# Second MoE product with w_out stationary, 144 tokens moving, and results turned by VectorE

## The chip, the cores and the metric

The kernel runs on one core of one Trainium2 chip. The metric is device microseconds (us) of one execution, and lower is better. A kernel is executed several times, always beside the kernel before on the same chip, and medians with their ranges are given. One execution of each kernel is profiled. Everything is fp32.

## The reference

Attention over pooled keys and values feeds a two-layer product, which the program calls `moe` (hence the title). Cut to what matters:

```python
# q, k, v: 8 batches x 8 heads x 576 x 64; k and v are averaged over 8 rows
attn = softmax(q @ k_p.T / 8);  x = (attn @ v_p) as (4608 tokens, 512)
h = x @ w_in                       # 512 x 2048: the first product
s = sin(alpha * h)
g = h + s * s / (alpha + 1e-9)
out = g @ w_out                    # 2048 x 512: the second product
```

The change concerns the last line, and how `g` and `w_out` are laid out for it.

## The kernel before

Both products use a two-level scheme of seven products in place of eight: a block product is split into 7 outer products of sums of blocks, each of these into 7 inner ones. Words used below:

- A **unit** is the piece of tokens that the second product finishes before it starts the next: 512 tokens, so 9 units.
- A **step** is one outer product: 7 inner products with four fp32 matmuls each. The profile shows two TensorE instructions per matmul, so a step has 56 and a unit 392.
- **Outer sums** are additions over whole 128x2048 blocks of `g`, four per unit. **Inner sums** are additions over quarters of such a block, four per step. VectorE makes both.
- The **bridge** is the buffer in HBM through which `g` goes from the first product to the second.

The data are stationary (first operand of `matmul`), 128 columns of weights move, and the outputs have tokens on partitions:

```python
def outer(u, n):                       # u: unit, n: step in it
    ...
    if n == 1: x[5] = new(5); tt(flat(x[5]), flat(r["r21"]), flat(x[4]), OP.add)
    if n == 2:
        x[6] = new(6); tt(flat(x[6]), flat(x[5]), flat(x[1]), OP.subtract)
        x[7] = r["r21"]; tt(flat(x[7]), flat(x[1]), flat(x[7]), OP.subtract)
    if n == 3: x[3] = new(3); tt(flat(x[3]), flat(x[2]), flat(x[6]), OP.subtract)

def inner(u, p):                       # the four inner sums of a step, made one step ahead
    ...
    tt(s1, a(2, 1), a(2, 2), OP.add)
    tt(s2, s1, a(1, 1), OP.subtract)   # product 6 of the step reads s2
    tt(s4, a(1, 2), s2, OP.subtract)
    tt(s3, a(1, 1), a(2, 1), OP.subtract)

def product(st, q, out, start):
    A, W = st["A"][q], self.W[st["p"]][q]
    for J in range(self.NJ):
        nc.tensor.matmul(out, A[:, J, :], W[:, J // 2, J % 2, :], ...)
...
for k in range(len(seq) + 1):          # one step; the order in which TensorE meets its products
    ...
    product(st, 1, yz[:, 0, :], True)
    ...                                # products 5 and 4 of the step before
    product(st, 6, x[:, 1, :], False)
    ...                                # products 2 and 3 of the step before, then its combination
    product(st, 7, x[:, 2, :], False)
...
self.load_g(0, ("r21",))
with tc.manual_schedule(engines={nc.tensor.engine}):   # only TensorE keeps the written order;
    for _ in o:                                        # a scheduler orders the other engines
        pass
```

A finished output block of 256 tokens x 256 columns goes to HBM in one store with rows of 1 KB.

Of the kernel before, what the change touches and what calls it, by code (L numbers as in the profile page):

```python
# [40 lines left out]
class Kernel:  # L41
    def __init__(self, tc, q, k, v, w_in, w_out, alpha, out):
        self.tc, self.nc = tc, tc.nc
        self.q, self.k, self.v = q, k, v
        self.w_in, self.w_out, self.alpha, self.out = w_in, w_out, alpha, out
        self.B, self.H, self.S, self.D = q.shape
        self.Sp = self.S // POOL
        self.DM = self.H * self.D
        self.FF = w_in.shape[1]
        self.K1 = self.DM // P  # L50
        self.K2 = self.FF // P
        self.NP = self.H // 2
        self.NU = self.B * self.S // (2 * TH)
        self.NJ = self.K2 // 2 // JW
        self.xT = {}
        self.gd = self.nc.dram_tensor("g_bridge", (self.NU, self.NJ, P, 4 * JW * TH), F32, kind="Internal").ap()

    def home(self, i, shape):

        return self.xp.tile(shape, F32, name=f"home{i}")  # L60
# [319 lines left out]
    def load_w_out(self, wp):  # L380


        nc, h, kk = self.nc, self.DM // 2, self.K2 // 2
        src = self.w_out.rearrange("(k p) n -> p k n", p=P)
        self.wb = {p: wp.tile([P, self.NJ, 2, 2, P], F32, name=f"wb{p}") for p in range(1, 8)}
        flat = lambda t: t[:].rearrange("p a b c d -> p (a b) (c d)")
        b11, b21, b22, t4, t1, t2, b12 = (flat(self.wb[p]) for p in range(1, 8))
        for t, i, j in ((b11, 0, 0), (b12, 0, 1), (b22, 1, 1), (b21, 1, 0)):
            nc.sync.dma_start(out=t, in_=src[:, i * kk:(i + 1) * kk, j * h:(j + 1) * h])
        for c in range(0, kk, 2):  # L390
            yield
# [7 lines left out]
        self.W = {}  # L399
# [5 lines left out]
    def inner_w(self, p, wp):  # L405
# [11 lines left out]
        tt(t1, b(1, 2), b(1, 1))  # L417
        tt(t2, b(2, 2), t1)
        tt(b(1, 2), b(2, 2), b(1, 2))
        tt(t4, b(2, 1), t2)  # L420
        self.W[p] = {1: b(1, 1), 2: b(2, 1), 3: b(2, 2), 4: t4, 5: t1, 6: t2, 7: b(1, 2)}

# [24 lines left out]
    def hidden(self, u, extra):  # L447
# [5 lines left out]
        for slot in range(7 * self.NJ):  # L453
# [5 lines left out]
            if k == 0:  # L459
                before = self.group  # L460
                G = self.group = SimpleNamespace(
                    u=u, J=J, b1=bank(), g=self.hp.tile([P, 2, 2, JW, TH], F32, name="h"),
                    s=self.hp.tile([P, 2, 2, JW, TH], F32, name="s", bufs=1))
# [11 lines left out]
            def sin(G, i, j, src):  # L475
                for jj in range(JW):
                    f = i * self.K2 // 2 + G.J * JW + jj
                    nc.scalar.activation(out=G.s[:, i, j, jj, :], in_=src[:, jj, :], func=AF.Sin, scale=self.al[:, f:f + 1])  # L478

            def square(G, i, js):  # L480

                for jj in range(JW):
                    f = i * self.K2 // 2 + G.J * JW + jj
                    x = G.s[:, i, js, jj, :]
# [33 lines left out]
            def left4(G=G):  # L518
                add(G.g[:, 1, 1], G.b7[:], G.p5[:])

            def left5(G=G):
                add(G.g[:, 0, 1], G.b6[:], G.p5[:])
                sin(G, 1, 1, G.g[:, 1, 1])
                add(G.g[:, 0, 0], G.b1[:], G.s[:, 0, 0])

            def left6(G=G):
                sin(G, 0, 1, G.g[:, 0, 1])
# [10 lines left out]
    def finish(self, Q):  # L538
        add = lambda o, x, y: self.nc.vector.tensor_tensor(out=o, in0=x, in1=y, op=OP.add)  # L539
        add(Q.g[:, 1, 0], Q.b7[:], Q.s[:, 1, 0])  # L540
        add(Q.g[:, :, 1], Q.g[:, :, 1], Q.s[:, :, 1])

    def store_g(self, Q):
        self.nc.sync.dma_start(out=self.gd[Q.u, Q.J], in_=Q.g[:].rearrange("p a b c d -> p (a b c d)"))
# [142 lines left out]

    def load_g(self, u, names):
        for n in names:
            i, j = divmod(("r11", "r12", "r21", "r22").index(n), 2)  # L690
            shape = [P, self.NJ, JW, 2, P]
            t = self.home(0 if n == "r22" else 2, shape) if n in ("r22", "r21") else self.gp.tile(shape, F32, name=n)
            self.nc.sync.dma_start(out=t[:].rearrange("p J a b c -> p J (a b c)"),
                                   in_=self.gd[u, :, :, (2 * j + i) * JW * TH:(2 * j + i + 1) * JW * TH].rearrange("J p c -> p J c"))
            self.R[n] = t

    def outputs(self):

        nc = self.nc
        ORDER = (1, 2, 4, 6, 7, 5, 3)  # L700
        flat = lambda t: t[:].rearrange("p J a b c -> p (J a b c)")
        tt = lambda o, x, y, op: nc.vector.tensor_tensor(out=o, in0=x, in1=y, op=op)  # L702
        X, C = {}, {}
        self.ne = False

        def outer(u, n):
# [4 lines left out]
            shape = [P, self.NJ, JW, 2, P]  # L711
            new = lambda p: self.home(3, shape) if p == 3 else self.gs.tile(shape, F32, name=f"x{p}")
# [4 lines left out]
            if n == 2:  # L717
                x[6] = new(6)
                tt(flat(x[6]), flat(x[5]), flat(x[1]), OP.subtract)
                x[7] = r["r21"]  # L720
                tt(flat(x[7]), flat(x[1]), flat(x[7]), OP.subtract)
            if n == 3:
# [3 lines left out]
        def inner(u, p):  # L726
            x = X[u][p]
            self.ne = not self.ne
            shape = [P, 4, self.NJ, P]
            e = self.gp.tile(shape, F32, name="xe") if self.ne else self.home(1, shape)  # L730
            a = lambda i, j: x[:, :, j - 1, i - 1, :]
            s1, s2, s3, s4 = (e[:, i] for i in range(4))
            tt(s1, a(2, 1), a(2, 2), OP.add)
            tt(s2, s1, a(1, 1), OP.subtract)
            tt(s4, a(1, 2), s2, OP.subtract)
            tt(s3, a(1, 1), a(2, 1), OP.subtract)
            return {1: a(1, 1), 2: a(1, 2), 3: s4, 4: a(2, 2), 5: s1, 6: s2, 7: s3}

        def product(st, q, out, start):
            A, W = st["A"][q], self.W[st["p"]][q]  # L740
            for J in range(self.NJ):
                nc.tensor.matmul(out, A[:, J, :], W[:, J // 2, J % 2, :], start=(start and J == 0), stop=(J == self.NJ - 1), skip_group_check=True)  # L742

        def block(n, bufs=1):
            return self.op.tile([P, 2, 2, P], F32, name=n, bufs=bufs)

        def combine(st):

            u, p, x, z = st["u"], st["p"], st["x"], st["yz"]
            c = C.setdefault(u, {})  # L750
            add = lambda o, a, b: tt(o, a, b, OP.add)
            x4 = x[:].rearrange("p (i j) c -> p i j c", i=2)
            z2 = z[:, 1:2, :].to_broadcast([P, 2, P])
            with_z = lambda t: add(t[:, :, 1, :], t[:, :, 1, :], z2)

            def out(i, j, t):
                r = u * 2 * TH + i * TH
                nc.sync.dma_start(out=self.out[r:r + TH, j * 2 * P:(j + 1) * 2 * P].rearrange("(t p) n -> p t n", p=P),
                                  in_=t[:].rearrange("p t j c -> p t (j c)"))
            if p in (1, 4, 5):  # L760
                t = c[p] = block(f"c{p}")
                nc.scalar.copy(out=t[:], in_=x4)
                with_z(t)
                if p == 5:
                    o = block("o", 4)
                    add(o[:], c[7][:], t[:])
                    out(1, 1, o)
                    c[3] = block("c3")
                    add(c[3][:], c[6][:], t[:])
            elif p in (2, 3):  # L770
                o = block("o", 4)
                add(o[:], c[1 if p == 2 else 3][:], x4)
                if p == 2:
                    with_z(o)
                out(0, 0 if p == 2 else 1, o)
            else:
                t = c[p] = block(f"c{p}")
                add(t[:], c[1 if p == 6 else 6][:], x4)
                with_z(t)
                if p == 7:  # L780
                    o = block("o", 4)
                    add(o[:], t[:], c[4][:])
                    out(1, 0, o)

        last = None
        seq = [(u, n) for u in range(self.NU) for n in range(7)]
        outer(0, 0)
        A = {(0, 0): inner(0, 1)}
        yield
        A[0, 1] = inner(0, 2)  # L790
        yield
        for k in range(len(seq) + 1):
            st = None
            if k < len(seq):
                u, n = seq[k]
                st = {"u": u, "p": ORDER[n], "A": A.pop((u, n))}
                if n in (2, 3):
                    outer(u, n)
                if n == 3 and u + 1 < self.NU:
                    self.load_g(u + 1, ("r11", "r12", "r22"))  # L800
                if n == 5 and u + 1 < self.NU:
                    self.load_g(u + 1, ("r21",))
                if n == 6 and u + 1 < self.NU:
                    outer(u + 1, 0)
                st["x"] = self.bank([P, 4, P])
                st["yz"] = self.ps_y.tile([P, 2, P], F32, name="ps_y", tag="y")
                x, yz = st["x"], st["yz"]
                product(st, 1, yz[:, 0, :], True)
                nc.scalar.copy(out=x[:, 0:2, :], in_=yz[:, 0:1, :].to_broadcast([P, 2, P]))  # L809
                if k == 0:  # L810
                    yield
            if last:
                product(last, 5, last["yz"][:, 1, :], False)
                product(last, 4, last["x"][:, 2, :], False)
                if last["p"] == 3:

                    t, z = C[last["u"]][3], last["yz"]
                    tt(t[:, :, 1, :], t[:, :, 1, :], z[:, 1:2, :].to_broadcast([P, 2, P]), OP.add)
            if st:
                product(st, 6, x[:, 1, :], False)  # L820
                nc.scalar.copy(out=x[:, 2, :], in_=x[:, 1, :])  # L821
                if k == 0:
                    yield
                if k + 1 < len(seq) and seq[k + 1] not in A:
                    A[seq[k + 1]] = inner(seq[k + 1][0], ORDER[seq[k + 1][1]])
                if u == 0 and n in (3, 4):
                    self.inner_w(ORDER[n + 2], self.gs)
            if last:
                product(last, 2, last["x"][:, 0, :], False)
                product(last, 3, last["x"][:, 1, :], False)  # L830
                combine(last)
            if st:
                product(st, 7, x[:, 2, :], False)
                nc.scalar.copy(out=x[:, 3, :], in_=x[:, 2, :])  # L834
                if n == 1:
# [101 lines left out]
```

## Time and profile before

| | before |
|---|---|
| time, median of the first 3 runs | 955.38 us (955.31 to 955.65) |
| span of the profiled execution (a run of 953.88 us) | 952.0 us |
| first to last matmul of the second product | 545.57 to 948.07 = 402.50 us |
| last matmul to the end of the span | 3.91 us |

In the profile PE stands for the matmuls of TensorE, PEld for its weight loads, DVE for VectorE, ACT for ScalarE, POOL for GpSimd, and SPq for the queue in which SyncE issues DMAs. The stretch's line in the table of stretches (stretch, length, busy time and instructions of PE, PEld, DVE, ACT and POOL, granted clock, DMA share, GB/s), and the stores of the outputs:

```profile
545.57:948.07 402.50, 401.98 (x3553) 399.64 (x3551) 299.80 (x421) 75.66 (x230) 0.00 (x0) 1.00 0.34 115
```

```profile
out_dram<-o SPq DMA_DIRECT2D x36, 256.0 KB
```

### The profile page before, as it was taken

Reading aid. Unit: us, or ns where it says so; the run is one execution under the profiler, and the core shown is the slowest. Engines: PE = TensorE matmul, PEld = TensorE weight load, DVE = VectorE, ACT = ScalarE, POOL = GpSimd, SP = SyncE. Lnnn points to the kernel's source line nnn. Section 1 sums busy time; section 2 is a strip of 40 time slices with the busy share of each in tenths; the row PEclk is TensorE's granted clock in tenths of the full one; section 3 lists DMA queues with packets and bytes.
Section 4 is the critical chain, followed back from the end, with each engine's and each line's share of the span. In section 5 each row is a group of like instructions: output and inputs, shape, how many; then the busy total and the mean of one; then the engine's idle time right before and its main releaser. Section 6 shows DMA issues by size and latency. Waiting matters only on the chain.

```text
span 952.0 us, 18201 instructions
## 1 busy us (share of the span) xinstructions
PE 932.7 (98%) x7251; PEld 830.2 (87%) x7251; DVE 659.0 (69%) x1025; ACT 440.2 (46%) x1026; POOL 199.7 (21%) x214
## 2 busy tenths in 40 slices
PE   5999999999999999999999999999999999999998
PEld 3687787887878788787888899999999999999998
DVE  5778574867748576583556996867868595958684
ACT  5478576675867758676666631111111111111111
POOL 1629363453625445260000000000000000000000
PEclk9999999999999999999999999999999999999999
DMA  9645457676577665636525144424142434333201
GB/s 227 181 142 165 149 160 201 185 168 190 152 189 210 142 178 124 190 115 204 205 89 206 66 179 148 145 89 156 67 155 80 145 121 145 105 129 123 101 34 34
DMA packets 84035, 137.86 MB, mean 145 GB/s; under 512 B 10176, under 2 KB 49872, under 8 KB 79344
## 3 DMA queue, kind: packets, MB, share of 16 engines
q1 hardware_dynamic: 83920, 136.70, 47.2%
q8 instruction: 58, 0.95, 0.4%
q14 instruction: 25, 0.20, 0.1%
q10 hardware_dynamic: 32, 0.01, 0.0%
HBM read 74.46 MB, written 47.19 MB: 128 GB/s over the span
## 4 chain that ended last, share of the span: by engine, by line
PE 95%; ACT 2%; DVE 1%; DMA 1%; issue 0%; SPq 0%; DVEq 0%; ACTq 0%
PE bank L472 45%; PE bank L742 30%; PE ps_y L742 12%; PE ps_o L309 3%; PE ps_sc L208 2%; DMA q<-in_q_dram 1%; PE ps_qt L189 1%; PE ps_at L267 1%; PE bank L435 1%; ACT s L478 0%; DVE as L371 0%; DVE home L445 0%; PE ps_or L318 0%; PE bank L120 0%; PE bank L208 0%
## 5 line engine op out<-in xcount | busy, mean ns | idle before, releaser
L472 PE MATMUL bank<-home,a 128*128 128x256 f32 x1152 | 267.1, 383 | 0.8 <-ACT bank L510 0.8
L472 PEld LDWEIGHTS bank<-home,a 128*128 128x128 f32 x1152 | 214.8, 190 | 35.5 <-ACT bank L510 2.7
L472 PE MATMUL bank<-home,as 128*128 128x256 f32 x864 | 202.4, 383 | 1.0 <-DVE as L371 0.8
L472 PEld LDWEIGHTS bank<-home,as 128*128 128x128 f32 x864 | 161.2, 190 | 26.2 <-ACT bank L498 3.0
L105 POOL TENSOR_TENSOR kvin<-kvin 72x512 f32<-72x512 f32 x112 | 123.8, 1105 | 163.5 <-DMA kvin<-in_v_dram 107.8
L485 ACT ACTIVATE s<-s,c 128x256 f32<-128x256 f32 (+1 forms) x216 | 110.0, 572 | 0.0
L478 ACT ACTIVATE s<-h,al 128x256 f32<-128x256 f32 x144 | 65.2, 501 | 82.0 <-DVE h L451 82.0
L451 DVE TENSOR_TENSOR h<-bank,p 128x512 f32<-128x512 f32 x72 | 49.0, 680 | 63.5 <-ACT s L485 28.1
L742 PE MATMUL bank<-wb,home 128*128 128x128 f32 x712 | 92.1, 275 | 0.0
L742 PEld LDWEIGHTS bank<-wb,home 128*128 128x128 f32 x712 | 85.7, 192 | 0.0
L821 ACT COPY bank<-bank 128x128 f32<-128x128 f32 x63 | 15.8, 250 | 149.1 <-PE bank L742 149.0
L478 ACT ACTIVATE s<-bank,al 128x256 f32<-128x256 f32 x144 | 59.9, 467 | 36.0 <-DVE h L539 9.5
L742 PE MATMUL bank<-wb,xe 128*128 128x128 f32 x512 | 67.6, 275 | 0.0
L742 PEld LDWEIGHTS bank<-wb,xe 128*128 128x128 f32 x512 | 62.4, 192 | 0.1
L834 ACT COPY bank<-bank 128x128 f32<-128x128 f32 x63 | 15.8, 250 | 96.9 <-PE bank L742 96.9
L539 DVE TENSOR_TENSOR h<-bank,s 128x512 f32<-128x512 f32 x36 | 24.6, 683 | 45.7 <-ACT s L485 45.0
L250 POOL TENSOR_TENSOR ex<-ex,sm 128x576 f32<-128x576 f32 (+1 forms) x38 | 42.7, 1148 | 58.6 <-ACT ex L239 24.4
L539 DVE TENSOR_TENSOR h<-h,s 128x1024 f32<-128x1024 f32 x36 | 45.8, 1273 | 0.0
L809 ACT COPY bank<-ps_y 128x256 f32<-128x256 f32 x63 | 22.5, 357 | 35.9 <-PE ps_y L742 35.9
L702 DVE TENSOR_TENSOR xe<-home 128x512 f32<-128x512 f32 x30 | 19.4, 686 | 26.1 <-PE bank L742 26.1
L145 DVE STREAM_TRANSPOSE tr<-q 128x1024 f32<-128x1024 f32 (+1 forms) x24 | 18.1, 808 | 26.8 <-DMA aT<-tr 21.3
L216 DVE TENSOR_TENSOR ex<-ps_sc,mx 128x288 f32<-128x288 f32 (+1 forms) x75 | 34.2, 456 | 2.9
(150 smaller groups left out, 1474.0 us busy)
## 6 DMA issues: line engine op xcount, KB each, us to landing
g_bridge<-h SPq DMA_DIRECT2D x36, 1024.0 KB
r<-g_bridge SPq DMA_DIRECT2D x18, 1024.0 KB
home<-g_bridge SPq DMA_DIRECT2D x18, 1024.0 KB
out_dram<-o SPq DMA_DIRECT2D x36, 256.0 KB
q<-in_q_dram SPq DMA_DIRECT2D x8, 1024.0 KB
kvin<-in_k_dram SPq DMA_DIRECT2D x28, 288.0 KB
kvin<-in_v_dram SPq DMA_DIRECT2D x28, 288.0 KB
a<-in_moe_w_in_dram SPq DMA_DIRECT2D x16, 256.0 KB
```

Of the source, the lines that this page charges most:

```text
L105: (eng or nc.gpsimd).tensor_tensor(out=o, in0=t[:, :, 0:w], in1=t[:, :, w:2 * w], op=OP.add)
L216: nc.vector.tensor_tensor(out=ex[:n, i, e::2, 0:Sp], in0=ps[:n], in1=mx[:n].unsqueeze(2).to_broadcast([n, NP, Sp]), op=OP.subtract)
L250: eng.tensor_tensor(out=E(n, i, 0, H), in0=E(n, i, 0, H), in1=sm[:n].unsqueeze(2).to_broadcast([n, H, Sp]), op=OP.mult)
L309: nc.tensor.matmul(ps[64 * e:64 * e + 64, :], vp[:, h, :], x, start=True, stop=True)
L451: add = lambda o, x, y: nc.vector.tensor_tensor(out=o, in0=x, in1=y, op=OP.add)
L472: nc.tensor.matmul(ps[:, jj, :], self.A[p][:, kk, f * P:(f + 1) * P], x[:, kk, :], start=(start and jj == 0 and kk == 0), stop=(kk == 1), ...
L478: nc.scalar.activation(out=G.s[:, i, j, jj, :], in_=src[:, jj, :], func=AF.Sin, scale=self.al[:, f:f + 1])
L485: nc.scalar.activation(out=x, in_=x, func=AF.Square, scale=self.c[:, f:f + 1])
L539: add = lambda o, x, y: self.nc.vector.tensor_tensor(out=o, in0=x, in1=y, op=OP.add)
L702: tt = lambda o, x, y, op: nc.vector.tensor_tensor(out=o, in0=x, in1=y, op=op)
L742: nc.tensor.matmul(out, A[:, J, :], W[:, J // 2, J % 2, :], start=(start and J == 0), stop=(J == self.NJ - 1), skip_group_check=True)
L809: nc.scalar.copy(out=x[:, 0:2, :], in_=yz[:, 0:1, :].to_broadcast([P, 2, P]))
```

## The change

The intent: each matmul has a fixed part and needs a weight load, and with 128 columns moving these cost most. Let weights be stationary and 144 tokens move, and the second product needs 8 units of 576 tokens in place of 9, with 3136 instructions in place of 3528. The outputs then have columns on partitions. VectorE turns them back in 32x32 blocks. To make 64 neighbouring output columns come out together, ScalarE permutes the columns of `w_out` as it is loaded. The bridge is laid out by feature, so that a unit of 576 tokens can be read from it. Besides, every engine now keeps the written order in the second product, the outer sums lie in four different steps, the inner sums are handed out over a step, and the first unit has an order of its own. Not in the cut below: the result of an outer product now lies in two banks of TensorE's output memory, many buffers are laid out anew, and ScalarE issues the load of one of the first unit's blocks. The core of the diff:

```diff
-        self.gd = self.nc.dram_tensor("g_bridge", (self.NU, self.NJ, P, 4 * JW * TH), F32, kind="Internal").ap()
+        self.T = self.S // 4
+        self.gd = self.nc.dram_tensor("g_bridge", (2, self.NJ * JW, P, self.B * self.S), F32, kind="Internal").ap()
 ... (load_w_out: eight-row pieces of w_out, 16 ScalarE copies that permute columns)
 ... (outer)
+            if n == 3:
                 x[7] = r["r21"]
                 tt(flat(x[7]), flat(x[1]), flat(x[7]), OP.subtract)
-            if n == 3:
+            if n == 4:
                 x[3] = new(3)
 ... (inner)
             tt(s1, a(2, 1), a(2, 2), OP.add)
             tt(s2, s1, a(1, 1), OP.subtract)
+            yield
+            tt(s3, a(1, 1), a(2, 1), OP.subtract)
+            yield
             tt(s4, a(1, 2), s2, OP.subtract)
 ... (product)
-                nc.tensor.matmul(out, A[:, J, :], W[:, J // 2, J % 2, :], ...)
+                nc.tensor.matmul(out, W[:, J // 2, J % 2, :], A[:, J, :], ...)
 ... (out, new)
+            nc.vector.transpose(out=o[:].rearrange("p n h c -> p h n c"), in_=...)
+            for a in range(4):
+                c = j * 2 * P + a * 64
+                nc.sync.dma_start(out=self.out[r:r + 2 * T, c:c + 64].rearrange("(n k) c -> k n c", k=32),
+                                  in_=o[32 * a:32 * a + 32].rearrange("k n h c -> k n (h c)"))
 ... (the loop over steps)
-                if n in (2, 3):
+                if 0 < n < 5 and k != 1:
                     outer(u, n)
 ... (run)
-            self.load_g(0, ("r21",))
-            with tc.manual_schedule(engines={nc.tensor.engine}):
+            with tc.manual_schedule(engines=engines):
+                self.load_g(0, ("r21",))
```

## The prediction

> **What bounds the kernel now.** I read the page's first and fourth parts, then the table of stretches, to see which engine sets the end and where.
>
> ```profile
> PE 932.7 (98%) x7251; PEld 830.2 (87%) x7251; DVE 659.0 (69%) x1025; ACT 440.2 (46%) x1026; POOL 199.7 (21%) x214
> ...
> PE 95%; ACT 2%; DVE 1%; DMA 1%; issue 0%; SPq 0%; DVEq 0%; ACTq 0%
> ```
>
> TensorE is busy 98% of the span, and the chain that ended last lies on it for 95%. So only what TensorE does per instruction, or how long it waits, can move the end. The second product runs from about 553 us to 948 us. One unit of 512 tokens in its steady part (columns: stretch, length, busy time and instructions of PE, PEld, DVE, ACT, POOL, clock, DMA share, GB/s):
>
> ```profile
> 700.30:744.35 44.05, 44.05 (x394) 43.90 (x393) 32.72 (x47) 7.76 (x25) 0.00 (x0) 1.00 0.36 120
> ```
>
> TensorE has no idle time there, and weight loads are busy for 43.90 of 44.05 us. In the page's groups the first product, with 256 columns moving, looks different:
>
> ```profile
> L472 PE MATMUL bank<-home,a 128*128 128x256 f32 x1152 | 267.1, 383 | 0.8 <-ACT bank L510 0.8
> L472 PEld LDWEIGHTS bank<-home,a 128*128 128x128 f32 x1152 | 214.8, 190 | 35.5 <-ACT bank L510 2.7
> ...
> L742 PE MATMUL bank<-wb,home 128*128 128x128 f32 x712 | 92.1, 275 | 0.0
> L742 PEld LDWEIGHTS bank<-wb,home 128*128 128x128 f32 x712 | 85.7, 192 | 0.0
> ```
>
> There loads are busy 215 of 267 us and have slack; in the second product nearly none. The question is whether the moving columns or the loads set the pace of the second product. The timeline answers (columns: start, time of the group, engine, instructions). Each fp32 product leaves two instructions; a group of n takes (n-1) paces plus one duration, so pace = (time - mean)/(n-1).
>
> ```profile
> 24.91 1.04 PE L267 MATMUL ps_at<-ident,ex 128*72 128x128 f32 x8
> ...
> 467.52 3.62 PE L472 MATMUL bank<-home,as 128*128 128x256 f32 x16
> ...
> 780.03 1.06 PE L742 MATMUL bank<-wb,xe 128*128 128x128 f32 x8
> ...
> 787.18 1.06 PE L742 MATMUL ps_y<-wb,x 128*128 128x128 f32 x8
> ```
>
> 256 columns: (3.62-0.383)/15 = 215.8 ns. 128 columns with 128-wide weights: eight groups of eight start between 780.03 and 787.18, so 7.15/64 = 111.7 ns. 128 columns with weights only 72 wide (a transpose): (1.04-0.273)/7 = 109.6 ns. If the columns alone set the pace, 128 columns would cost 215.8 - 128/1.2 = 109.1 ns, which the narrow weights nearly show; the wide ones cost some 2.5 ns more. I read this as: **at 128 columns the 128-wide weight load sets the pace, by a hair**, and the change leaves that corner.
>
> **What the Trainium skill says.** "TensorE: Matmul & The Clock Gate", section "LDWEIGHTS (loading the stationary operand)": a load costs its column count over 1.2 (106.7 ns for 128), whatever the rows. The same page, "Back-to-back issue gap": spacing is set by both operations together, and an isolated gap is N/2.4 + 2.5 ns. Here an fp32 instruction shows twice the slope: 256/1.2 + 2.5 = 215.8, exactly the measured pace; 128/1.2 + 2.5 = 109.2 against 111.7 measured. So the form agrees with N doubled, and the surplus at 128 fits the load. "VectorE: DVE Perf Modes", "The three transpose paths": VectorE turns only 32x32 blocks, which is why the output columns are permuted in the weights. "DMA: Bandwidth & Descriptors", "Specifications": below 512 B a write is a read-modify-write. The outputs become 256 B runs; the trace before has no such writes to HBM that I could size.
>
> **The change part by part.**
>
> *TensorE.* Before: 9 units x 49 products x 8 instructions = 3528 at 128 columns. After: 8 x 49 x 8 = 3136 at 144. Columns streamed are equal (451,584); what is saved is the fixed part and the load's surplus. Pace at 144: 144/1.2 + 2.5 = 122.5 ns, above the load's 111.7. A unit then takes 392 x 122.5 = 48.02 us. The unit before should be 392 x 111.7 = 43.79 and was 44.05, so some 0.3 us of small waits per unit; I keep them: 48.3 us. Stage: 9 x 44.05 = 396.5 before, 8 x 48.3 = 386.4 after: **-10 us**, all on the path.
>
> *VectorE.* It is beside TensorE. Costs from these rows:
>
> ```profile
> L702 DVE TENSOR_TENSOR home<-home,home 128x512 f32<-128x512 f32 x4 | 2.7, 685 | 0.0
> ...
> L702 DVE TENSOR_TENSOR c<-c,ps_y 128x256 f32<-128x256 f32 x6 | 2.5, 412 | 0.0
> L702 DVE TENSOR_TENSOR x<-home,home 128x2048 f32<-128x2048 f32 x1 | 2.3, 2293 | 1.2 <-PE bank L742 1.2
> ...
> L276 DVE STREAM_TRANSPOSE tr<-ex 128x768 f32<-128x768 f32 x24 | 21.9, 948 | 0.0
> ```
>
> Slope about 1.04 ns per element: 288 elements cost 0.445 us, 576 cost 0.75, 2304 cost 2.55; a turn of 576 about 0.71. The built program has per unit 31 operations of 576, 4 of 2304, 15 of 288 (the product is now in two banks, so adds are split) and 4 turns: 23.3 + 10.2 + 6.7 + 2.8 = 43.0 us, less some 0.07 us by which consecutive ones overlap, 54 times: 39 us of 48, 81% (74% before). The worst step is the third product of a unit: 2.5 us for the outer sum, 2.7 for the inner sums, 1.8 for the output block with its turn, 7.0 us against a step of 56 x 122.5 = 6.9 us. The last inner sum then falls some 1.5 us into the next step, but its product stands about 5 us into it. So VectorE runs late, not too late.
>
> *ScalarE.* About 8.7 us of 48 per unit. Sixteen copies of 128x512 that permute w_out (near 0.6 us each) fall into the eighth hidden unit, where ScalarE is about 65% busy; I expect under 0.5 us on the path.
>
> *DMA.* Bridge loads keep their bytes in 1,152 B runs, outputs go in 256 B runs: 4,608 x 8 = 36,864 packets. The stage's DMA share, 0.36, should rise to 0.5 to 0.7. Next unit's blocks are asked for in the fourth step and needed from the seventh on, some 18 us for the first 1.2 MB. Hidden.
>
> *The tail.* Exposed. The last matmul group ends at 947.01 + 1.06 = 948.07, the span at 951.98: 3.9 us, made of one add and this one issue and its landing:
>
> ```profile
> 948.16 0.69 DVE L702 TENSOR_TENSOR o<-c,bank 128x512 f32<-128x512 f32 x1 [1.63 <-PE bank L742]
> 948.87 0.37 SPq L758 DMA_DIRECT2D out_dram<-o  x1
> ```
>
> After: an add of 288 (0.445), a turn (0.71), then four issues instead of one: +0.47 us, and three more issues at 0.37 to 0.6 us: **+2 us**.
>
> Sum: 955.4 - 10.1 + 2.0 + 0.5 (hand-over between the products) = 947.8; I say 948.
>
> **Rivals.** (1) *Straight line between the two paces*: 111.7 + 16 x (215.8 - 111.7)/128 = 124.7 ns, that is, the surplus at 128 is a fixed cost and not the load. Stage 8 x (392 x 124.7 + 300) = 393.5 us, a gain of 3 us that the tail nearly eats: 954 to 955. For it: only two sizes are seen with full-width weights. Against: the narrow-weight case lies on the other line. (2) *VectorE becomes the bound*: it is the engine that gains work, now in a fixed order on every engine. If the sums came late by 0.3 us in each of 56 steps, 17 us would be lost and the kernel be slower by 1%. Against: the margins above. (3) *Short output writes crowd out the bridge loads*: then TensorE would wait at a unit's start for the first block, 1 to 3 us a unit, 8 to 24 us in all. Against: 0.36 share now, 18 us lead. (4) *Nothing seen*: load and columns interfere further at 144 and the gain stays under 2 us.
>
> **Range and chances.** The pace carries 10 us of gain with some 70% in my judgement, 3 us otherwise; tail and hand-over together can be off by 2 us. That gives 944.5 to 955. Two per cent is 19 us: twice the gain I can find on the path, and no rival against it looks likely to cost that. Faster 2%, same 96%, slower 2%.
>
> **What would show it right or wrong.** Groups of eight at 144 columns 0.98 us apart: pace right; 1.00 us: rival 1. Weight loads busy near 89% of the stage instead of 99.7%. A TensorE wait released by a VectorE sum inside a unit: rival 2; by a bridge load: rival 3. From the last matmul to the end about 6 us. The prediction is wrong if waits of TensorE in the stage exceed a few us, or the pace is not near 122.5 ns.

## More of the kernel before

Call the time from the first to the last matmul of the second product **the stretch**.

## The result, and the profile after

| | before | after |
|---|---|---|
| time, median (range, runs) | 955.35 us (954.6 to 955.65, 4) | 943.38 us (943.17 to 943.62, 4) |
| ratio | | 0.9876, 95% interval 0.9859 to 0.9893 |
| span of the profiled execution | 952.0 us | 941.8 us |
| the stretch | 402.50 us | 390.18 us |
| last matmul to the end | 3.91 us | 5.72 us |

A ratio here is the mean time of one kernel's runs over that of the other's in the same rounds, so it is not quite the ratio of the medians in the table. The change is 1.2% faster, which counts as "same" at 2%. The time lies 1.1 us below the predicted range.

The page of the changed kernel, its first and fourth parts:

```profile
PE 920.8 (98%) x6859; PEld 819.5 (87%) x6859; DVE 694.5 (74%) x1043; ACT 445.6 (47%) x1042; POOL 197.9 (21%) x214
...
PE 94%; DVE 2%; ACT 2%; DMA 1%; issue 0%; SPq 0%; ACTq 0%; DVEq 0%
```

TensorE still carries the end, with 392 instructions fewer. The largest groups of the second product:

```profile
L778 PE MATMUL bank<-s,wb 128*128 128x144 f32 x896 | 119.4, 286 | 0.4 <-ACT bank L891 0.4
L778 PEld LDWEIGHTS bank<-s,wb 128*128 128x128 f32 x896 | 113.7, 190 | 0.7 <-ACT bank L891 0.6
```

One matmul takes 286 ns from start to modelled end, but that is not its pace. The timeline (start, time of the group, engine, instructions) gives the pace:

```profile
734.03 1.14 PE L778 MATMUL ps_y<-s,a 128*128 128x144 f32 x8
735.01 1.14 PE L778 MATMUL bank<-x,as 128*128 128x144 f32 x8
735.99 1.14 PE L778 MATMUL bank<-s,we 128*128 128x144 f32 x8
```

Groups of eight start 0.98 us apart, and (1.14 - 0.286)/7 = 0.122 us: the predicted 122.5 ns. The table of stretches, first the whole stretch, then a window as long as two units in the steady part:

```profile
545.90:936.08 390.18, 389.77 (x3161) 388.71 (x3159) 332.94 (x439) 73.66 (x230) 0.00 (x0) 1.00 0.41 117
700.00:796.04 96.04, 96.04 (x787) 96.04 (x786) 82.47 (x109) 16.93 (x55) 0.00 (x0) 1.00 0.46 124
```

Units begin at 695.81, 743.83 and 791.85 us, so one takes 48.02 us, which is 392 x 122.5 ns to the hundredth: there is no gap left inside a unit after the first. In the whole stretch, 390.18 - 3136 x 0.1225 - 5.2 = 0.8 us of waiting remain, where it was 3.2 us. So the stretch became 12.3 us shorter: **9.9 us by the matmuls themselves, 2.4 us by waits that went away**. Of these 2.4 us, read from start times, 2.1 lay in the eight units after the first and 0.3 to 0.4 in the first.

What the waits of before were is to be seen in its timeline, in one of the first steps of a unit (the first three lines are TensorE, the others VectorE):

```profile
731.30 1.06 PE L742 MATMUL ps_y<-we,xe 128*128 128x128 f32 x8
732.19 1.06 PE L742 MATMUL bank<-we,r 128*128 128x128 f32 x8
733.24 1.13 PE L742 MATMUL bank<-we,home 128*128 128x128 f32 x8
...
728.67 2.28 DVE L702 TENSOR_TENSOR x<-x,r 128x2048 f32<-128x2048 f32 x1
...
732.41 0.68 DVE L702 TENSOR_TENSOR home<-home,r 128x512 f32<-128x512 f32 x1
```

The groups should start 0.89 us apart, and the second and third are 1.05 apart. The third reads the inner sum `s2`, which ends at 732.41 + 0.68 = 733.09, 0.15 us before it starts. VectorE had worked without a break since an outer sum of 2.28 us, which the scheduler had put in front of it; that this sum is the cause is tested below. Such gaps of 0.05 to 0.15 us, about 0.27 us in a unit, are too short for the list of waits. For TensorE in this stretch it names only one wait in either kernel, the first line before, the second after (what waits, what for, us in total, times, longest):

```profile
PE bank L742 <- ACT bank L834: 0.4, 1, 0.4
PE bank L778 <- ACT bank L891: 0.4, 1, 0.4
```

This is the hand-over from the first product, and it costs the same in both. The gaps show only in start times.

What was paid at the end, in the timeline of the changed kernel:

```profile
936.11 0.45 DVE L733 TENSOR_TENSOR cc<-cc,bank 128x288 f32<-128x288 f32 x1 [0.32 <-PE bank L778]
936.60 0.78 DVE L796 STREAM_TRANSPOSE o<-cc 128x576 f32<-128x576 f32 x1
937.40 1.85 SPq L801 DMA_DIRECT2D out_dram<-o  x4
```

An add, a turn, and four issues of 0.32, 0.46, 0.47 and 0.47 us with short gaps; the data have landed 2.54 us after the last issue. Before, one add of 0.69 us, one issue of 0.37 us and a landing of some 2.7 us. The tail is 5.72 - 3.91 = 1.8 us longer. Together that is -12.3 + 1.8 = -10.5 us. The two profiled spans differ by 10.2 us, because in the second one the stretch began 0.3 us later.

The stores themselves:

```profile
out_dram<-o SPq DMA_DIRECT2D x128, 72.0 KB
```

### The profile page after: what moved, and what is told of

It reads as the page before. It is cut to its first block, busy times and chain, and to the rows that moved or that the text cites. A ratio compares the mean times of both kernels' runs of the same rounds, so it can differ in the third digit from the quotient of the medians. Undisturbed runs are those within 1.5% of the kernel's fastest.

```text
span 941.8 us, 17546 instructions
## 1 busy us (share of the span) xinstructions
PE 920.8 (98%) x6859; PEld 819.5 (87%) x6859; DVE 694.5 (74%) x1043; ACT 445.6 (47%) x1042; POOL 197.9 (21%) x214
## 4 chain that ended last, share of the span: by engine, by line
PE 94%; DVE 2%; ACT 2%; DMA 1%; issue 0%; SPq 0%; ACTq 0%; DVEq 0%
PE bank L497 45%; PE bank L778 29%; PE ps_y L778 12%; PE ps_o L311 3%; PE ps_sc L210 2%; DMA q<-in_q_dram 1%; DVE as L373 1%; PE ps_qt L191 1%; PE ps_at L269 1%; ACT s L503 1%; PE bank L460 1%; DVE home L470 0%; PE ps_or L320 0%; PE bank L122 0%; DVE a L373 0%
## 5 line engine op out<-in xcount | busy, mean ns | idle before, releaser
L778 PE MATMUL bank<-s,wb 128*128 128x144 f32 x896 | 119.4, 286 | 0.4 <-ACT bank L891 0.4
L778 PEld LDWEIGHTS bank<-s,wb 128*128 128x128 f32 x896 | 113.7, 190 | 0.7 <-ACT bank L891 0.6
L891 ACT COPY bank<-bank 128x144 f32<-128x144 f32 x56 | 14.7, 263 | 145.7 <-PE bank L778 144.3
L503 ACT ACTIVATE s<-bank,al 128x256 f32<-128x256 f32 x144 | 59.9, 467 | 33.5 <-PE bank L497 10.5
L910 ACT COPY bank<-bank 128x144 f32<-128x144 f32 x56 | 14.7, 263 | 88.2 <-PE bank L778 88.2
L733 DVE TENSOR_TENSOR s<-r 128x576 f32<-128x576 f32 x64 | 48.1, 752 | 0.8
L733 DVE TENSOR_TENSOR s<-x 128x576 f32<-128x576 f32 x48 | 36.2, 753 | 7.6 <-PE ps_y L778 6.7
L868 ACT COPY bank<-ps_y 128x288 f32<-128x288 f32 x56 | 21.4, 383 | 38.7 <-PE ps_y L778 38.7
L778 PE MATMUL bank<-s,a 128*128 128x144 f32 x256 | 36.6, 286 | 0.0
L778 PE MATMUL ps_y<-s,a 128*128 128x144 f32 x256 | 36.6, 286 | 0.0
```

The source lines that it names most:

```text
L503: nc.scalar.activation(out=G.s[:, i, jj, j, :], in_=src[:, jj], func=AF.Sin, scale=self.al[:, f:f + 1])
L733: tt = lambda o, x, y, op: nc.vector.tensor_tensor(out=o, in0=x, in1=y, op=op)
L778: nc.tensor.matmul(out, W[:, J // 2, J % 2, :], A[:, J, :], start=(start and J == 0), stop=(J == self.NJ - 1), skip_group_check=True)
L868: nc.scalar.copy(out=x0[:], in_=yz[:, 0:1, :].to_broadcast([P, 2, T]))
```

## The experiments

The theories at the start: **(pace)** the gain is the matmul pace of 122.5 ns over fewer instructions, and the load's hold on 128 columns is what made those dear; **(order)** the rest of the gain is waits that the new order of VectorE's work removed, whatever the size of the unit. The rivals: the turned operands or the new bridge made something faster in themselves; or the better order was the fixed order on all engines by itself, not where the sums lie in it; or the size of the unit alone took the waits away because a longer step leaves VectorE more time. All runs gave correct results. "Before" is the kernel before on the same chip.

### The changed kernel again, twice

No edit: it shows how well the result stands on other chips.

> The changed kernel as it is, as the reference for the other runs on this chip. Theory A (pace 122.5 ns at 144 columns against 111.7 ns at 128, and no waits of TensorE for VectorE's sums inside a unit): 943.4 us again, 12 us under the kernel before. Theory C (1.5 us of the 12 are the kernel before itself, whose timed runs were 955.3 us and whose profiled run was 953.9 us): the kernel before shows timed runs as low as 954 us here, and the difference falls to about 10.5 us.

> The changed kernel as it is once more, beside the next run on one chip. From the first matmul of the second product to the end of the last: 390.18 us again, as on two chips so far; time 943 to 944 us.

| chip | before, median (range, runs) | after, median (range, runs) | ratio (95% interval) |
|---|---|---|---|
| second | 954.17 us (953.52 to 955.09, 9) | 943.85 us (943.61 to 944.32, 4) | 0.9892 (0.9879 to 0.9906) |
| third | 954.49 us (953.27 to 954.99, 7) | 942.89 us (942.5 to 944.2, 4) | 0.9886 (0.987 to 0.9903) |

The gain of the medians is 10.3 and 11.6 us, and 12.0 us on the first chip; on the second chip it is what theory C expected. The stretch of the changed kernel was 390.18 us in all three profiles, beginning at 545.90, 546.64 and 544.82 us. The spread of a microsecond or two from run to run therefore lies ahead of it, in the attention and the first product. No gain of the change shows there: over all the profiles below the stretch begins between 545.13 and 546.70 us with the first product of before, and between 544.82 and 546.64 with that of the changed kernel.

### All of the change but the size of the unit

```diff
-        self.T = self.S // 4
+        self.T = TT                                # TT = 128
+        self.US = 4 * self.T                       # tokens of a unit, used in load_g and out
+        self.UN = self.B * self.S // self.US       # 9 units, used in the loop over steps
```

> The changed kernel with 128 tokens moving and units of 512 tokens (nine), everything else of the change kept. Theory A (the load of 128 columns sets the pace at 128): pace 111.7 ns, 3528 instructions, 394.1 us of matmuls instead of 384.2, so 9 to 10 us slower than the changed kernel: 953 us. Theory D (the gain comes from having w_out stationary, not from the size): pace near 109.2 ns, 385.3 us of matmuls, 944.5 us.

952.74 us (951.87 to 953.01, 5 runs) against 954.17: ratio 0.9984 (0.9971 to 0.9996). Its stretch, and two groups of its timeline:

```profile
545.44:945.52 400.08, 399.68 (x3553) 398.64 (x3551) 338.79 (x493) 77.42 (x257) 0.00 (x0) 1.00 0.40 116
```

```profile
735.42 1.06 PE L781 MATMUL ps_y<-r,wb 128*128 128x128 f32 x8
736.31 1.06 PE L781 MATMUL ps_y<-s,we 128*128 128x128 f32 x8
```

This splits the gain cleanly. The groups are 0.89 us apart, the pace of the kernel before, with operands swapped: so turning the operands makes no matmul faster. The stretch is 402.5 - 400.1 = 2.4 us shorter than before without any change of size, and the units after the first have no gaps. From this kernel to the changed one, only the size differs, and the stretch loses 400.1 - 390.2 = 9.9 us. The waits are gone at 128 tokens too, so the longer step is not needed to remove them. That a longer step could also do it by itself is not ruled out by this run (see the run with only TensorE in the written order).

### The pace by itself

Twelve fp32 matmuls of each size, one row after another, were added behind the changed kernel, with nothing but TensorE in them; the total time says nothing here.

```diff
+PACES = [(128, n) for n in (96, 112, 120, 128, 132, 136, 144, 160, 192, 256)] + [(m, 128) for m in (72, 96, 120)]
+                for M, N in PACES:
+                    ps = self.bank([P, 512])
+                    for j in range(12):
+                        nc.tensor.matmul(ps[0:M, 0:N], w[:, P * j:P * j + M], x[:, 0:N], start=(j == 0), stop=(j == 11), skip_group_check=True)
```

> The changed kernel with a row of extra fp32 products after its last one, on TensorE alone, into unused banks: twelve products (24 instructions) each with 128-wide weights and 96, 112, 120, 128, 132, 136, 144, 160, 192, 256 columns moving, then 128 columns moving with weights 72, 96 and 120 wide. Theory A (pace is the larger of the load, 111.7 ns for 128 weight columns, and N/1.2 + 2.5 ns): 111.7 ns for 96, 112, 120 and 128 columns, 112.5 for 132, 115.8 for 136, 122.5 for 144, 135.8 for 160, 162.5 for 192, 215.8 for 256; 109.2 ns at 128 columns with the narrower weights. Theory D (a fixed cost per instruction, straight line): 85 ns for 96, 105 for 120, 111.7 for 128, 118 for 136, 124.7 for 144, and no gain from narrower weights.

978.57 us. Mean distance of the starts of the instructions, worked out from the trace; the first distance of each row is left out, because where the rows meet it differs (82 ns at 96 columns, 115 to 125 ns at 112 to 132):

| columns moving, weights 128 wide | 96 | 112 | 120 | 128 | 132 | 136 | 144 | 160 | 192 | 256 |
|---|---|---|---|---|---|---|---|---|---|---|
| ns | 111.7 | 111.7 | 111.7 | 111.6 | 112.5 | 115.9 | 122.5 | 135.9 | 162.5 | 215.9 |

With 128 columns and weights 72, 96 or 120 wide it was 109.1 ns each time. From 132 columns on the figures are N/1.2 + 2.5 (112.5, 115.8, 122.5, 135.8, 162.5, 215.8). From 96 to 128 columns the pace does not depend on the columns; there the load of 128-wide weights sets it, at 111.7 ns, and with narrower weights the 128 columns fall back to 109.1, near their own 109.2. The pace theory holds, as **the larger of load and columns**. How the load's own limit falls with narrower weights is not seen, since the 128 columns already bound those rows; the profile's record of a single load does get shorter, 190, 183, 163 and 143 ns for weights 128, 120, 96 and 72 wide. The two lines cross near 131 columns. At 144 columns TensorE pays 122.5/144 = 0.851 ns per column, at 128 columns 111.7/128 = 0.873, a saving of 2.5%, and 2.5% of 394.1 us are the 9.9 us.

Units of 768 tokens (192 columns) would pay 0.846 ns per column, 0.5% less than 144, but that size has no run: with 192 columns the program of the section before does not build, since a buffer of 30 KB per partition is wanted and 17.1 KB are left.

### The kernel before with all engines in the written order

```diff
-            self.load_g(0, ("r21",))
-            with tc.manual_schedule(engines={nc.tensor.engine}):
+            with tc.manual_schedule(engines=engines):
+                self.load_g(0, ("r21",))
```

> The kernel before, with the order of all engines in the second product fixed by hand as the program has it; tiles, units and matmuls unchanged. Theory B (order alone removes the waits): pace stays at 111.7 ns, the 0.27 us per unit go, 2 us under the kernel before in units after the first. Theory B': the waits stay, time within 0.5 us of the kernel before.

968.03 us (967.34 to 968.98, 4 runs), ratio 1.0144 (1.0129 to 1.016): slower by 14 us, and both expectations were missed. The waits of TensorE in the second product:

```profile
PE ps_y L742 <- DVE x L702: 5.8, 9, 0.6
PE bank L742 <- DVE home L702: 3.1, 5, 0.6
PE bank L742 <- DVE xe L702: 2.5, 4, 0.6
```

As written, the second step of a unit ends with one outer sum and the third begins with two: three in a row, nearly 7 us of VectorE's time, ahead of the inner sums that TensorE needs next. By start times, each unit after the first now waits 1.7 us, in the third step. In the timeline of before, a single one of 2.28 us stood ahead of the late inner sum. So a fixed order is no gain in itself, which refutes that rival. That the place of the sums counts is tried next.

### The kernel before, in written order, with its outer sums spread

First over three steps, with two sums together in one of them; then, after the result, over four, as in the changed kernel. The second edit on top of the last one:

```diff
+            if n == 3:
                 x[7] = r["r21"]
                 tt(flat(x[7]), flat(x[1]), flat(x[7]), OP.subtract)
-            if n == 3:
+            if n == 4:                     # the first version kept n == 3 here
                 x[3] = new(3)
...
-                if n in (2, 3):
+                if n in (2, 3, 4) or n == 1 and u:     # first version: (2, 3)
                     outer(u, n)
...
-                if n == 1:
+                if n == 1 and u == 0:
                     outer(u, 1)
```

> The kernel before with all engines' order in the second product fixed by hand as in the failed attempt, but with the outer sums spread over the unit: one at the start of the second product, one in the third, two in the fourth, instead of three in a row. Theory B (the late sums are a matter of the order, not of VectorE's load): no gaps between matmuls inside a unit after the first, so the 0.27 us per unit of the kernel before go; 44.05 us per unit becomes 43.8, and the time 1 to 2 us under the kernel before, unless the first unit's waits grow. Theory B' (with 128 columns the step is too short for the sums): gaps of some tenths of a us stay in each unit.

Three steps: 955.38 us (954.02 to 956.55, 6 runs) against 955.16, ratio 1.0002 (0.999 to 1.0015). The gaps went from 0.27 to 0.12 us per unit, all of them behind the step with two sums, but the first unit waited 1.8 us longer, and the stretch was 403.18 us. The time was not 1 to 2 us under the kernel before, as theory B had it.

> The kernel before with all engines' order in the second product fixed by hand and the four outer sums in four different steps, as in the changed kernel; tiles, 128 columns, units of 512 and the direct output unchanged. With two of them in one step, gaps of 0.12 us per unit were left, behind the step with the two. Theory B (a late inner sum behind outer sums that stand close together): no gaps over 4 ns inside units after the second; from the fourth unit on 43.78 us per unit (392 x 111.7 ns) against 44.05. Theory B' (VectorE too slow for 128 columns): 0.1 us or more of gaps per unit stay.

Four steps: 953.79 us (952.61 to 955.06, 5 runs) against 953.89, ratio 0.9999 (0.9985 to 1.0012). A window as long as two units in the steady part:

```profile
700.00:787.56 87.56, 87.56 (x787) 87.56 (x786) 69.22 (x92) 15.51 (x48) 0.00 (x0) 1.00 0.35 121
```

Each unit after the first takes 43.77 us from start to start, and 392 x 111.7 ns are 43.79 us: the gaps inside units are gone, with nothing changed but the places of the outer sums and the fixed order. With the order fixed alone the unit took 45.50 us, with the sums over three steps 43.90. That is the order theory shown for the steady part, 2.1 of the 2.4 us. Yet the stretch is 402.37 us, as long as before, and 3.1 us of waiting are still in it: the list of waits now has two waits for VectorE in the first unit, of 1.1 and 0.6 us, beside the hand-over of 0.4 us. What the steady units won was given back at the start. The changed kernel does not pay this, and it is the one with an order of its own in the first unit. Which piece of that order does it was not tried.

### The changed kernel with only TensorE in the written order

```diff
-            with tc.manual_schedule(engines=engines):
+            with tc.manual_schedule(engines={nc.tensor.engine}):
```

> The changed kernel, but in the second product only TensorE's order is fixed by hand, as in the kernel before; the other engines' order is the scheduler's. Theory B (the order of VectorE's sums removed the 0.27 us of waits per unit that the kernel before shows): about 2 us slower than the changed kernel, 945 to 946 us, with gaps over 126 ns between matmuls once or twice per unit. Theory B' (the waits went because a step is now 6.86 us long and not 6.25, whatever the order): within 0.5 us of the changed kernel, no such gaps.

948.70 us (948.23 to 949.31, 5 runs), ratio 0.9942 (0.993 to 0.9955) against 0.9892 of the changed kernel on that chip: 4.9 us of the gain lost. Both theories missed the time. For the steady part B' was right: from 605 us on, where the second unit begins, each unit takes 48.02 us and there is no wait at all. All is lost in the first unit, and this is the largest piece, in the timeline (in brackets the idle time ahead of an instruction and what ended it):

```profile
566.91 2.56 DVE L733 TENSOR_TENSOR x<-r,r 128x2304 f32<-128x2304 f32 x1 [2.02 <-DMA r<-g_bridge]
...
572.36 1.25 PE L778 MATMUL ps_y<-x,wb 128*128 128x144 f32 x8 [2.81 <-DVE x L733]
```

VectorE stands still for a block of the bridge to land, then makes the outer sum, and TensorE waits 2.81 us for what follows. So at 144 tokens the fixed order matters at the start of the second product, where the scheduler's choice was poor, and not in the steady part. Why the scheduler's order is good enough there is open. It may be the longer step, or the new places and buffers of the sums, since no run has the changed kernel at 128 tokens with the scheduler's order.

### One and two additions too many on VectorE

The prediction's second rival was VectorE as the bound. Useless additions of 128x576 show how far away it is.

```diff
+            for _ in range(EXTRA if st else 0):       # EXTRA = 1, then 2
+                j = self.op.tile([P, 4 * T], F32, name="junk")
+                f = lambda p: self.wb[p][:].rearrange("p a b c d -> p (a b c d)")[:, 0:4 * T]
+                add(j[:], f(1), f(2))
```

> The changed kernel with one useless VectorE addition of 128x576 (0.75 us) more per step in the second product, ahead of the last inner sum. If VectorE has the margin that the prediction works out (it runs up to 1.5 us late where some 5 us are free): VectorE goes from 85% to near 95% busy, and the time stays within 0.5 us of the changed kernel. If VectorE is nearly the bound (rival 2): waits of TensorE for sums appear in the steps with outer sums, and the kernel is 5 us or more slower.

One per step: 945.90 us (944.99 to 946.75, 4 runs), ratio 0.9901 (0.9885 to 0.9917). The changed kernel was not run on that chip, but the stretch can be compared: 392.55 us against 390.18, so 2.4 us more, where at most 0.5 or at least 5 had been expected. All of it is three waits in the first two units (0.5, 1.2 and 0.4 us, each with 0.1 us after it; the next expectation says three units, which the start times do not bear out). The same window as above:

```profile
700.00:796.04 96.04, 96.04 (x786) 96.04 (x785) 90.56 (x123) 16.93 (x54) 0.00 (x0) 1.00 0.44 124
```

VectorE is busy 90.56 of 96.04 us, 94%, and TensorE still loses nothing in these units.

> The changed kernel with two useless VectorE additions of 128x576 more per step in the second product. One more put VectorE at some 95% and cost 2 us, all in the first three units. With two, VectorE's work per step is about 41 + 14 x 0.68/7 x 7 = 50.5 us per unit against 48.0 us of matmuls: TensorE must now wait in every unit, 2 to 3 us each, some 15 to 20 us in all, 960 us. If waits stay confined to the first units, the bound of VectorE is farther off than its busy share says.

Two per step: 975.43 us in one look, worse than the 960 that were expected. A stretch of 100 us, and the two main waits:

```profile
700.00:800.00 100.00, 94.03 (x761) 93.17 (x760) 97.77 (x132) 16.30 (x53) 0.00 (x0) 1.00 0.40 109
```

```profile
PE ps_y L779 <- DVE r L734: 14.4, 8, 1.8
PE ps_y L779 <- DVE x L734: 10.4, 8, 1.9
```

VectorE is busy 97.77 of 100 us, and TensorE waits twice in each unit. From the third unit on a unit takes 51.55 us, 3.5 more than its matmuls. So VectorE is the bound with two additions per step and not with one. The steady units of the changed kernel, at 86%, have room for one more such operation in each step, not for two; the first two units have none.

### The tail: part of the last block turned and sent early

Of the last block's 288 tokens, one half is finished before the last two products, and 128 of these fill whole 32x32 blocks. They can be turned and stored early, and the rest, 160, at the end, with two engines issuing.

```diff
+            if st["u"] == self.B - 1:
+                st["o"] = out(st["u"], 0, 1, t, blocks=(5, 9))     # second version: issued by ScalarE
...
+                if u == self.B - 1:
+                    out(u, 0, 1, t, o=st["o"], blocks=(0, 5), engines=(nc.sync, nc.scalar))
```

> The changed kernel with the end alone altered: of the last block of results, the 128 tokens that are complete early are turned and sent early; the other 160 are turned at the end and their four stores are issued by two engines. If the longer end (5.7 us from the last matmul to the end, against 3.9 before) is made of the turn and of four issues one after another at 0.46 us: 0.3 us less turn and 0.9 us less issuing, 1.2 us under the changed kernel. If the landing of the short runs is what takes the time: under 0.3 us.

> As the split end tried before, but the early part's four stores are issued by ScalarE, so that SyncE has only the block before and two of the last stores to issue. In the first attempt SyncE was still issuing until 939.2 us, 2.1 us before the end, so nothing was won. If issuing one after another is what makes the end long: last issue 1.5 us sooner, the end some 4.3 us after the last matmul and not 5.7, 1 to 1.5 us under the changed kernel. If it is the landing: no change.

The first version: 943.34 us (942.83 to 943.57, 4 runs), ratio 0.9876 (0.9863 to 0.9889), on a chip where the changed kernel was not run. Its tail is 5.81 us against 5.72, so nothing is won. SyncE issued early stores until 937.5 us, then waited 0.9 us for a store to land, and its last issue ended at 939.2 us. The second leaves the early stores to ScalarE: 943.07 us (942.28 to 943.12, 4 runs), ratio 0.9882 against 0.9886 of the changed kernel in the same rounds, tail 5.33 us. 0.4 us are won in the trace, where 1 to 1.5 were expected, and nothing that the times can show. The trace tells what stood in the way. The block was turned at 937.01 us, but ScalarE issued early stores until 937.97, and SyncE's first store of the last four left only at 937.74. The list of SyncE's waits has this:

```profile
SPq L805 <- DMA out_dram<-o: 2.1, 2, 1.7
```

SyncE waited for earlier stores to land. Its two last stores have the same semaphores (counters that tell of a landing) as two of the early stores. These landed at 937.68 and 938.20 us, and the last stores left at 937.74 and 938.22. Stores with semaphores of their own were not tried. The last issue ended at 938.96 us, 1.95 us after the turn, where in the changed kernel it ended 1.87 us after it. No version beat the changed kernel.

## Why the prediction was right or wrong

The expected time was 948.0 us, with a range down to 944.5; the measured one is 943.38 us. The mechanism of the pace and the largest term were right. The step that failed is the term of the waits.

- **Pace: right.** 122.5 ns predicted, 122.5 measured, in the kernel and in the row of sizes. The matmuls gave 9.9 us, as worked out. Rival 1, the straight line with 124.7 ns, is refuted, and so is rival 4, a gain under 2 us.
- **Waits: wrong, and this is the miss.** The step was "so some 0.3 us of small waits per unit; I keep them: 48.3 us", with 0.5 us more for the hand-over. The 0.3 us were read correctly off the unit of before, but they were taken as a toll of TensorE. They had a cause, the outer sums in front of the inner ones, and the change removes it by where it puts the outer sums (shown with the kernel before; in the changed kernel the longer step may help too). A unit took 48.02 us. The 0.5 us for the hand-over did not come either: it waits 0.4 us by the list, before and after. The prediction's sum had the waits grow by 0.4 us (0.5 for the hand-over, less 0.1 for one unit fewer); they shrank by 2.4 us. That is 2.8 us of the 4.6 us between the expected and the measured time. I had read the change's order of VectorE only as a risk, never as a gain; the range below 948 had room for nothing of the kind but the tail.
- **Tail: right.** 2 us predicted, 1.8 measured: 0.2 us more of the miss. The landing after the last issue was not longer with short runs.
- **The base: a part that is only argued.** Rounding 947.8 up to 948 is 0.2 us of the miss. The remaining 1.4 us or so are not seen in the stretch or the tail. The traces give -10.5 us, and from 955.38 us that would have been 944.9 us, inside the range. The kernel before has run medians from 953.89 to 955.35 us, and the prediction started at the upper end; from their middle, 954.5, the traces give 944.0 us. With the gain of the second chip, 10.3 us, the result would have been inside the range; so whether it fell just outside was in part chance.
- **The start: misread, without harm.** The prediction has the second product run from about 553 us; its first matmul is at 545.57. No sum rests on it.
- **Weight loads "near 89% busy": wrong as a sign.** The prediction does not say how it came to 89%. In the two units above they are busy 96.04 of 96.04 us, although they no longer set the pace. A load takes 190 ns on the page and overlaps its neighbours, so the union of loads fills the time. The group times and the pace told the truth, the busy share did not.
- **VectorE: too low, without harm.** 81% predicted, 82.47 of 96.04 us = 86% measured. The turn took 0.78 us, not 0.71:

```profile
L796 DVE STREAM_TRANSPOSE o<-cd 128x576 f32<-128x576 f32 x2 | 1.6, 778 | 0.1
```

  The larger part is the overlap of consecutive operations, for which I took off 54 x 0.07 = 3.8 us a unit; 41.2 us measured per unit leave about 2. Rival 2 did not come: no wait for VectorE inside a unit. In the steady units it is more than one, and less than two, additions of 576 per step away.
- **ScalarE and the permuting copies: right.** In the 60 us from 440 to 500 us, where the copies lie, ScalarE's busy time rose from 38.98 to 46.37 us and TensorE stayed at 59.91 us.
- **DMA: too high, without harm.** The stage's share rose from 0.34 to 0.41, where 0.5 to 0.7 was predicted. No wait for a bridge load, so rival 3 did not come.

## What to carry to other kernels

The pace of a row of matmuls is the larger of the weight load and the moving columns, so choose the moving size past the point where the columns take over; far beyond it little more is to be had (0.851 ns per column at 144, 0.843 at 256). Read the pace from start times, not from busy shares. When a steady stage takes a little more than instructions times pace, do not carry the rest over as a constant: find the operand that is late, and ask whether the change moves the work that makes it late. Where a scheduler and a fixed order differ, count where long operations lie in front of short ones that the bottleneck needs, and look at the first unit apart from the steady ones.

## What the Trainium skill lacked or had wrong

- "TensorE: Matmul & The Clock Gate", "Back-to-back issue gap": that section has no figures for fp32. Here an fp32 matmul leaves two instructions, each N/1.2 + 2.5 ns from the next: 122.5 ns at 144 columns, 162.5 at 192, 215.9 at 256. The page says of its formula that it counts too much at large N in a real stream of loads and matmuls; with the slope doubled it held in such a stream to 0.1 ns, from 132 up to 256 columns; more were not run.
- The same page, "LDWEIGHTS (loading the stationary operand)" and "Back-to-back issue gap": it says that both operations set the spacing, but not how. The runs show the larger of the two: 111.7 ns for 96 to 128 columns with weights 128 wide, 109.1 ns for 128 columns with weights 72 to 120 wide. Where loads of 128 set the pace, it was 5 ns above the 106.7 that the page's formula gives as an estimate.
- "Trainium Kernel Development and Optimization", "Performance Expectations", calls the busy share of weight loads a good metric for how close a kernel is to its roofline. It does not tell what sets the pace: in the steady part the time covered by loads was 43.90 of 44.05 us where the load set it, and 96.04 of 96.04 us where it did not.
- "VectorE: DVE Perf Modes", "The three transpose paths": that section gives only a bf16 128x128 turn. An fp32 turn of 128x576 in 32x32 blocks took 0.78 us, beside 0.75 us for an addition of that size.
- "DMA: Bandwidth & Descriptors", "Specifications": writes below 512 B are said to be read-modify-writes. 36.9 thousand packets of 256 B to HBM took 18 ns each in the median, where packets of 1,024 B had taken 47 ns. That is 1.5 times as long per byte, which fits, but no wait of TensorE was for a DMA. The price on the path lay elsewhere: one store per block became four, at 0.32 to 0.47 us of issue each, one after another at the end.
